# q's last two rows in two transfers, and two fillers ahead of v's first transposes

## The chip, the core and the metric

The kernel runs on one core of one Trainium2 chip. Its metric is the device time of one execution in microseconds (us); a result is the median of several runs. The engines are called PE (matrix products), PEld (its loads of weights), DVE (vector), ACT (activation functions), POOL and SP; POOL and SP are used here above all to issue transfers (DMAs).

## What is computed

A cross-covariance attention over channels, for four batches, feeds a layer with a squared ReLU. All inputs are float32 (tau is 1):

```python
B, N, C = (4, 6080, 256)            # q, k, v
n_tokens, d_model, d_ff = (24320, 256, 2048)

def _attn_ref(q, k, v, tau) -> np.ndarray:
    qn = q / (np.linalg.norm(q, axis=1, keepdims=True) + 1e-06)
    kn = k / (np.linalg.norm(k, axis=1, keepdims=True) + 1e-06)
    s = kn.transpose(0, 2, 1) @ qn / tau
    s = s - s.max(-1, keepdims=True)
    a = np.exp(s)
    a /= a.sum(-1, keepdims=True) + 1e-09
    return (v @ a).astype(np.float32)

def _moe_ref(x, w_in, w_out, s, b) -> np.ndarray:
    h = x @ w_in
    r = np.maximum(h, 0.0)
    g = s * (r * r) + b
    return (g @ w_out).astype(np.float32)
```

The norms of q and k run over the 6080 rows of a batch, so they, and the 256 x 256 matrix of exponentials, are known only when the last row of q and of k has been read.

## The kernel before

**In outline.** For every batch, the Gram matrix of q and k is summed on PE (`mm`, L174, into s_ps), the squares of q and k are summed for the norms, the exponentials eT are formed, and the product of eT with w_in, called wa, replaces w_in; then h = v times wa, in groups of 512 tokens: v is transposed (vT), h_ps is made on PE (L825; for the first half of the first group L812), ACT takes the ReLU (L835), the squares are taken on DVE or ACT (L848, L846), and the second product follows (L996 with seven products in place of eight, L900 for the first and the last group). The Gram matrices of batches 1 to 3 are worked in between the groups of the batch ahead. Batch 0 has nothing to lie beside: its q and k are loaded and summed at the start, and this is where the change is.

**Batch 0 in pieces.** The 6080 rows are cut into 13 chunks: eleven of 128 partitions x 4 rows, and the last 448 rows as two chunks of 112 partitions x 2 rows. The first six come in pairs (`load_pair`), four by `load` (chunks 6 to 9). The last three chunks, which the code calls c0, c1 and c2 (10, 11, 12), are loaded in an order of their own (L547 to L549): k of c0, k of c1 and c2 together, q of c0 in two transfers of two rows a partition, q of c1 and c2 in two transfers of two rows a partition. In the last of these steps (`load_last(1)`, L158) the first transfer is q of c1 and the second q of c2. The transfers turn float32 into float16 on the way, so that a row of 256 is 512 bytes in the tile.

**The queue.** All these transfers are issued by POOL, in program order, and behind them v's first group without its last row a partition (`load_v(0, slice(0, 3))`, L557), w_in's first 256 columns and the next 256 (L558, L559), v's last row (L560), the rest of w_in in four pieces, v of group 1, w_out in four pieces, and so on.

**The end of batch 0's sums.** For c0, c1 and c2 `norm_ops` gives a list: the squares of k, the squares of q, and two steps that hand the squares, unfolded, to the sums. The squares of q of these chunks run on DVE (L201). In c0 the entry of q is itself a list of two, one a transfer; in c1 and c2 it is one function over both rows. `add_norms(0)` sums the squares of q over the partitions on PE, by products with a vector of ones, two a row (L270). The order on PE and DVE is written out by hand from L611 to L650: the squares and sums of k, k's inverse norms on ACT (`inverse_k`, four activations at L291), c0's and c1's products and sums for q, then for c2: the square of q (L641), the Gram products of its row 0 (L642), the hand-over, the last sums (`norms_q`, L644), the Gram products of row 1 (L645). Then come `inverse_q` (four activations on ACT, L291) and `scale_s` (two operations on DVE, L316), the transposes of v's first three rows a partition (`turn_v(0, range(3))()`, L648: six on PE at L496 and a copy to vT on DVE at L498), `keep_busy(1)` (L649) and `first_block`.

**The first block.** `first_block` (L354) forms the exponentials in two halves on ACT (L322). With each half PE makes the row sums r_ps (L362) and the first 256 columns of wa (L367). Then come the next 256 columns (L372), the transposes of v's fourth row, the reciprocal of the row sums on DVE (L378), and the scalings of wa: by ACT (L343) for one half of the rows of wa, by DVE (L345) for the other. The first h products (L812) read both.

**The fillers.** `keep_busy(n)` (L586) issues n products of a constant tile of ones, 128 x 512 float32, into a tile of PSUM that nobody reads (idle_ps, L589). It takes its tile from the pool of two that h_ps and the first wa_ps come from. Three fillers stand further ahead, behind chunks 7 and 8 (`FILL`, L584).

Of the kernel before, what the change touches and what calls it, by code (L numbers as in the profile page):

```python
# [16 lines left out]
def kernel(  # L17
# [37 lines left out]
    def po(ins):  # L55

        tc.keep_in_program_order(ins)
        return ins
# [32 lines left out]
    def h_tile(name):  # L91
        return ps_h.tile([P, 2, TG], FP32, tag="h_ps", name=name)


    JC = 4
# [16 lines left out]
    class Gram:  # L112
# [35 lines left out]
        def load_last(self, i):  # L148

            c = len(self.chunks) - 2  # L150
            at, np_, _ = self.chunks[c]
            if i == 0:
                self.raw[c] = qk_pool.tile([P, 2, JC, C], FP16, tag="qk", name="qk")
                for h in range(2):
                    t = self.raw[c][:, :, ts(h, 2)]
                    self.tiles[c + h] = t[:, 1], t[:, 0]
            rows = (k, q)[i][self.b, at:].rearrange("(p j) c -> p j c", j=JC)
            for js in [slice(0, JC)] if i == 0 else [ts(h, 2) for h in range(2)]:  # L158
                po(nc.gpsimd.dma_start(out=self.raw[c][:np_, i, js], in_=rows[:, js]))

        def cast(self, c):
# [21 lines left out]
        def norm_ops(self, c):  # L183

            qc, kc = self.tiles[c]
            _, np_, jc = self.chunks[c]
            st = {}

            at_end = self.b == 0 and c >= len(self.chunks) - NLATE

            def squares(a, js):
                def f():
                    if "sq" not in st:
                        if at_end:
                            st["sq"] = late_pool.tile([P, 2, jc, C], FP16, tag=f"sq{c}", name="sq")
                        else:
                            st["sq"] = sq_pool.tile([P, 2, JC, C], FP16, tag="sq", name="sq")
                    src = (qc, kc)[a][:np_, js, :]
                    if (a == 0 or c == len(self.chunks) - 1 if at_end else
                            a == 0 and (self.b > 0 or c % 2 == 0)):  # L200
                        po(nc.vector.tensor_mul(st["sq"][:np_, a, js, :], src, src))  # L201
                    else:
                        po(nc.scalar.activation(  # L203
                            out=st["sq"][:np_, a, js, :], in_=src, func=AF.Square))
                return f

            def fold(half, arrays, last):
                def f():
                    src = st["f", 2 * half] if 2 * half < jc else st["sq"]
                    if ("f", half) not in st:  # L210
                        if last:
                            t = f3_pool.tile([P, 2, 1, C], FP16, tag="f3", name="f3")
                        else:
                            t = sq_pool.tile([P, 2, half, C], FP16, tag=f"f{half}", name="f")
                        st["f", half] = t
                    po(nc.vector.tensor_add(  # L216
                        st["f", half][:np_, arrays], src[:np_, arrays, :half, :],
                        src[:np_, arrays, half : 2 * half, :]))
                    if last and c == 0:
                        self.first = st["f", half]  # L220
                    if last and c == 0:
                        for rows in self.rows:
                            rows.append((st["f", half], np_, 1))
                return f

            def into_first():

                dst, src = self.first[:np_], st["f", 1][:np_]
                if self.b == 0:
                    po(nc.vector.tensor_add(dst, dst, src))  # L230
                else:
                    po(nc.gpsimd.dma_start(out=dst, in_=src, accum_op=ALU.add))  # L232

            def unfolded(a):
                self.rows[a].extend((st["sq"][:, :, j : j + 1], np_, 1) for j in range(jc))

            if self.b == 0 and c >= len(self.chunks) - NLATE - 1:
                ops = [lambda i=i: unfolded(i) for i in range(2)]
                if c == len(self.chunks) - NLATE:
                    return [squares(1, slice(0, jc)), [squares(0, ts(h, 2)) for h in range(2)], *ops]  # L240
                return [squares(1, slice(0, jc)), squares(0, slice(0, jc)), *ops]
            ops = []
            for h in range(0, jc, 4):
                js = slice(h, min(h + 4, jc))
                ops += [squares(1, js), squares(0, js)]
            if jc == 8:
                ops += [fold(4, slice(0, 1), False), fold(4, slice(1, 2), False)]
            ops += [fold(2, slice(0, 2), False), fold(1, slice(0, 2), True)]
            return ops + [into_first] if c > 0 else ops
# [239 lines left out]
    def turn_v(g, js):  # L489
        v16 = v_tiles[g]  # L490
        if g not in vT_tiles:
            vT_tiles[g] = vtpool.tile([P, CH, TG], FP16, tag="vT", name="vT")
        vT_ps = ps_o.tile([P, CH, TG], FP16, tag="o_ps", name="vT_ps")
        for j in js:
            for ch in range(CH):
                po(nc.tensor.transpose(vT_ps[:, ch, ts(j, P)], v16[:, j, ts(ch, P)], ident16))  # L496
        cols = ds(js[0] * P, len(js) * P)
        return lambda: po(nc.vector.tensor_copy(out=vT_tiles[g][:, :, cols],  # L498
                                                in_=vT_ps[:, :, cols]))
# [86 lines left out]
    def keep_busy(n):  # L586

        for _ in range(n):
            po(nc.tensor.matmul(h_tile("idle_ps")[:, 0, :], fill[:, :P], fill, start=True,  # L589
                                stop=True, skip_group_check=True))  # L590
# [4 lines left out]
    for c in range(NCH0 - NLATE - 1):  # L595
        ops = g0.norm_ops(c)
# [7 lines left out]
    c_, c0, c1, c2 = range(NCH0 - NLATE - 1, NCH0)  # L604
    ops = {c: g0.norm_ops(c) for c in (c_, c0, c1, c2)}

    def add_rows(a, c):
        ops[c][2 + a]()
        g0.add_norms(a)
# [28 lines left out]
    g0.rows[0].extend(half)  # L638
    g0.add_norms(0)
    add_rows(0, c1)  # L640
    ops[c2][1]()  # L641
    g0.mm(c2, 0)  # L642
    ops[c2][2]()
    norms_q()  # L644
    g0.mm(c2, 1)  # L645
    for f in (*inverse_q, scale_s):
        f()
    turn_v(0, range(3))()  # L648
    keep_busy(1)  # L649
    first_block()  # L650


# [367 lines left out]
    for s in range(NS + FT):  # L1020
# [27 lines left out]
        squares = {**SQUARES, 3: (), 5: SQUARES[3], 7: SQUARES[5]} if g == 1 else SQUARES  # L1048
# [44 lines left out]
```

## Time and profile before

| what | before |
|---|---|
| median of 3 runs | 713.3 us (713.22 to 713.45) |
| the profiled execution, its own time | 713.27 us |
| its span, first to last instruction | 711.5 us |
| mean granted clock of PE | 0.998 |
| PE busy | 692.5 us (97% of the span) |
| DVE, ACT, POOL busy | 633.6 us (89%), 548.6 us (77%), 113.3 us (16%) |
| granted clock of PE, 23.51 to 26.93 us | 0.50 |
| granted clock of PE, 26.93 to 40.58 us | 1.00 |
| bytes moved, mean rate | 83.81 MB, 118 GB/s |
| rate from 26 to 34 us | 192 to 213 GB/s |

The profile is that of one execution, which took 713.27 us by the clock of the runs and 711.5 us from its first to its last instruction. Its views are used as follows. The chain that ended last is followed back from the last instruction to whatever released each step; it tells what a step waited for, on the assumption of one releaser each. The timeline has one line for an instruction or a few alike: start, length, engine, line, operation, the tile it writes and those that it reads, shapes, how many, and in brackets the idle time of the engine ahead of it with its releaser. The issues of transfers have the time from issue to landing. In the page, the line of PE's clock and of the engines' shares by slices of the span shows that the first slice (17.8 us) and the second are the only ones in which PE is not nearly full.

From issue to landing, for the transfers that matter (one issue each, asked for its own moment):

| transfer | issued at, us | KB | us to landing |
|---|---|---|---|
| q of c0, first two rows | 22.29 | 128 | 9.0 |
| q of c0, last two rows | 23.52 | 128 | 8.4 |
| q of c1 (first transfer of `load_last(1)`) | 24.76 | 112 | 7.8 |
| q of c2 (second) | 26.08 | 112 | 7.0 |
| v of group 0, three rows a partition | 27.31 | 192 | 7.8 |
| w_in, columns 0 to 255 | 28.53 | 128 | 6.8 |
| w_in, columns 256 to 511 | 29.79 | 128 | 6.2 |
| v of group 0, last row a partition | 30.89 | 64 | 5.4 |

### The profile page before, as it was taken

The numbers are of one execution on the slowest core, as the hardware profiler recorded it, in microseconds if no ns is written. First come the engines' busy times: TensorE is split into PE (matmuls) and PEld (weight loads), VectorE is DVE, ScalarE is ACT, GpSimd is POOL, SyncE is SP. The second block draws the span as 40 slices with busy tenths as digits, with TensorE's granted clock in tenths as the row PEclk, the third lists the DMA queues.
The fourth block names the chain that finished last, engine by engine and source line by source line (L and its number), as shares of the span: only waits on it lengthen the run. The fifth ranks groups of instructions, "written<-read, shape, count | busy, mean of one in ns | idle before, by whom it ended". The sixth has DMA issues, their size and how long they took to land.

```text
span 711.5 us, 17551 instructions
## 1 busy us (share of the span) xinstructions
PE 692.5 (97%) x7436; PEld 503.3 (71%) x7436; DVE 633.6 (89%) x904; ACT 548.6 (77%) x599; POOL 113.3 (16%) x189
## 2 busy tenths in 40 slices
PE   3799999999999999999999999999999999999998
PEld 2566777776777777777677777777768777777777
DVE  3899999999988989998999899998998888887886
ACT  5889877787787777778877777777877777877875
POOL 3543142202102221111010222111000000000000
PEclk9999999999999999999999999999999999999999
DMA  9999999657656979465771887838323323321202
GB/s 240 205 254 152 191 174 144 124 92 121 126 119 109 136 137 156 95 95 104 153 127 51 148 147 143 125 75 108 93 62 75 98 67 76 99 59 47 82 31 75
DMA packets 87694, 83.81 MB, mean 118 GB/s; under 512 B 56320, under 2 KB 63280, under 8 KB 87360
## 3 DMA queue, kind: packets, MB, share of 16 engines
q0 software_dynamic: 26848, 43.74, 38.5%
q1 hardware_dynamic: 60336, 37.71, 23.7%
q8 instruction: 58, 0.95, 0.6%
q10 hardware_dynamic: 432, 1.25, 0.5%
q14 instruction: 20, 0.16, 0.1%
HBM read 78.91 MB, written 24.90 MB: 146 GB/s over the span
## 4 chain that ended last, share of the span: by engine, by line
PE 95%; DMA 4%; ACT 1%; DVE 0%; issue 0%
PE h_ps L825 46%; PE o_ps L996 40%; PE s_ps L174 4%; DMA qk<-in_k_dram 1%; PE wa_ps L419 1%; DMA raw<-in_q_dram 1%; DMA v<-in_v_dram 1%; PE o_ps L900 1%; PE o_ps L872 0%; PE wa_ps L350 0%; ACT sq L203 0%; ACT qk L165 0%; DVE f L216 0%; PE vT_ps L496 0%; PE h_ps L812 0%
## 5 line engine op out<-in xcount | busy, mean ns | idle before, releaser
L835 ACT ACTIVATE r<-h_ps 128x1024 f16<-128x1024 f32 (+1 forms) x384 | 388.8, 1014 | 144.3 <-PE h_ps L825 141.1
L825 PE MATMUL h_ps<-vT,wa 128*128 128x512 f16 (+7 forms) x1628 | 450.9, 364 | 0.0
L996 PEld LDWEIGHTS <-S 128*128 128x128 f16 x2944 | 198.1, 98 | 84.3
L996 PEld LDWEIGHTS <-g 128*128 128x128 f16 x2208 | 155.0, 98 | 74.1
L848 DVE TENSOR_TENSOR g<-r 128x2048 f16<-128x2048 f16 (+2 forms) x150 | 174.4, 1163 | 10.2 <-ACT r L835 9.7
L996 PE MATMUL o_ps<-T,S 128*128 128x128 f16 x2208 | 183.1, 219 | 0.0
L825 PEld LDWEIGHTS <-wa 128*128 128x128 f16 x1628 | 136.3, 98 | 18.2 <-ACT wa L343 0.2
L996 PE MATMUL o_ps<-w_out,g 128*128 128x128 f16 x1472 | 134.2, 219 | 0.0
L846 ACT ACTIVATE g<-r 128x1024 f16<-128x1024 f16 (+1 forms) x97 | 100.3, 1034 | 0.2
L853 DVE SCALAR_TENSOR_TENSOR o_sb<-o_ps,s_out,u 128x256 f32<-128x256 f32 x138 | 66.2, 480 | 36.0 <-PE o_ps L996 34.4
L174 PE MATMUL s_ps<-qk 128*128 128x256 f16 (+1 forms) x384 | 71.1, 287 | 14.7 <-ACT qk L165 10.9
L485 POOL DMA_DIRECT2D v<-in_v_dram x49 | 32.4, 665 | 243.2 <-DMA vT<-v 150.2
L232 POOL DMA_DIRECT2D f<-f x33 | 28.9, 875 | 242.3 <-DVE f L216 188.9
L853 DVE SCALAR_TENSOR_TENSOR u<-o_ps,s_out,rowconst 128x256 f32<-128x256 f32 x138 | 65.7, 476 | 0.0
L996 PE MATMUL o_ps<-w_out,S 128*128 128x128 f16 x736 | 63.5, 219 | 0.0
L996 PE MATMUL o_ps<-N,g 128*128 128x128 f16 x736 | 63.4, 219 | 0.0
L925 DVE TENSOR_TENSOR S<-S,g 128x2048 f16<-128x2048 f16 (+1 forms) x47 | 56.4, 1200 | 1.2
L203 ACT ACTIVATE sq<-qk 128x1024 f16<-128x1024 f16 (+2 forms) x53 | 54.5, 1041 | 2.8 <-DVE f L216 1.8
L923 DVE TENSOR_TENSOR S<-g 128x2048 f16<-128x2048 f16 (+1 forms) x47 | 56.0, 1192 | 0.0
L929 DVE TENSOR_TENSOR S<-g,S 128x2048 f16<-128x2048 f16 x46 | 55.8, 1214 | 0.0
L927 DVE TENSOR_TENSOR S<-g 128x2048 f16<-128x2048 f16 x46 | 55.8, 1214 | 0.0
L174 PEld LDWEIGHTS <-qk 128*128 128x128 f16 (+1 forms) x384 | 32.9, 103 | 20.0 <-ACT qk L165 10.9
(108 smaller groups left out, 332.5 us busy)
## 6 DMA issues: line engine op xcount, KB each, us to landing
out_dram<-o_sb SPq DMA_DIRECT2D x41, 512.0 KB, 3.0
v<-in_v_dram POOLq DMA_DIRECT2D x46, 256.0 KB, 4.7
qk<-in_k_dram POOLq DMA_DIRECT2D x38, 256.0 KB, 6.3
qk<-in_q_dram POOLq DMA_DIRECT2D x37, 256.0 KB, 7.0
f<-f POOLq DMA_DIRECT2D x30, 128.0 KB, 3.2
out_dram<-o_sb SPq DMA_DIRECT2D x12, 256.0 KB, 4.3
vT<-v SPq DMA_TRANSPOSE x182, 3.4
w<-in_moe_w_out_dram POOLq DMA_DIRECT2D x4, 512.0 KB, 8.5
```

Source lines behind the costliest of these rows:

```text
L174: po(nc.tensor.matmul(self.s_ps[:, ch, :], qc[:np_, j, ts(ch, P)], kc[:np_, j, :], start=(c == 0 and j == 0 and ch == 0), stop=(c == len(s ...
L203: po(nc.scalar.activation(out=st["sq"][:np_, a, js, :], in_=src, func=AF.Square))
L825: po(nc.tensor.matmul(dst, wa[:, ci, ts(m, P)], src, start=(ci == 0), stop=(ci == CH - 1), skip_group_check=True))
L835: po(nc.scalar.activation(out=r16[:, :, i % 2, :n], in_=h_tiles.pop((g, i))[:, :, :n], func=AF.Relu))
L846: po(nc.scalar.activation(out=dst, in_=src, func=AF.Square))
L848: po(nc.vector.tensor_mul(dst, src, src))
L853: po(nc.vector.scalar_tensor_tensor(out=dst, in0=src, scalar=s_out, op0=ALU.mult, in1=add, op1=ALU.add))
L923: po(nc.vector.tensor_add(T[1], A21, A22))
L925: po(nc.vector.tensor_sub(T[2], T[1], A11))
L927: po(nc.vector.tensor_sub(T[3], A11, A21))
L929: po(nc.vector.tensor_sub(T[4], A12, T[2]))
L996: po(nc.tensor.matmul(st[name][:, j, :], a()[:, i, ts(j, P)], w[:, i, :], start=first, stop=last, skip_group_check=True))
```

## The change

q's part of `load_last` is issued as three transfers: rows 0 and 1 of a partition together as before, row 2 alone, row 3 alone. So q of c2 comes in two transfers of 112 partitions x 1 row. The squares of q of c2 become a list of two functions, one a row, which are called one after the other in the place where the one stood. The filler behind the transposes of v's first part goes away, and two fillers are issued ahead of `inverse_q`, `scale_s` and these transposes, behind the Gram products of c2's row 1.

```diff
@@ load_last
             rows = (k, q)[i][self.b, at:].rearrange("(p j) c -> p j c", j=JC)
-            for js in [slice(0, JC)] if i == 0 else [ts(h, 2) for h in range(2)]:
+            for js in [slice(0, JC)] if i == 0 else [slice(0, 2), slice(2, 3), slice(3, 4)]:
                 po(nc.gpsimd.dma_start(out=self.raw[c][:np_, i, js], in_=rows[:, js]))
@@ norm_ops
                 if c == len(self.chunks) - NLATE:
                     return [squares(1, slice(0, jc)), [squares(0, ts(h, 2)) for h in range(2)], *ops]
+                if c == len(self.chunks) - 1:
+                    return [squares(1, slice(0, jc)), [squares(0, ts(h, 1)) for h in range(2)], *ops]
                 return [squares(1, slice(0, jc)), squares(0, slice(0, jc)), *ops]
@@ the order by hand
     add_rows(0, c1)
-    ops[c2][1]()
+    for f in ops[c2][1]:
+        f()
     g0.mm(c2, 0)
     ops[c2][2]()
     norms_q()
     g0.mm(c2, 1)
+    keep_busy(2)
     for f in (*inverse_q, scale_s):
         f()
     turn_v(0, range(3))()
-    keep_busy(1)
     first_block()
```

## The prediction

> **What bounds the kernel now.** I read the chain that ended last first, the waits of the tensor engine second, and then the timeline of the start. By the page's chain, PE holds 95% of the span; the list of waits, asked for PE from 37 us to the end, comes back empty, and PE is busy for the whole of 40.58 to 700 us. So from about 37 us on PE waits for nobody: whatever moves the first matmuls of the feed-forward part moves the end by the same amount, and nothing behind them has time to give. The change lies wholly ahead of that point. The chain there, from the window 26 to 39 us (columns: start, length, what):
>
> ```profile
> 16.36 10.67 DMA qk<-in_k_dram
> 27.03 0.28 issue
> 27.31 7.77 DMA v<-in_v_dram
> 35.08 0.05 issue
> 35.13 0.51 PE vT_ps L496 x6
> 35.63 0.29 PE idle_ps L589
> 35.92 0.04 PE r_ps L362 x2
> ```
>
> v's first part lands at 35.08, six transposes follow, then one filler (L589, 0.29 us), then the first products with the exponentials. But a second chain runs beside this one, that of q's last rows. The timeline (start, length, engine, line, operation, count, idle before and its releaser):
>
> ```profile
> 32.54 0.98 DVE L201 TENSOR_TENSOR sq<-qk 112x512 f16<-112x512 f16 x2 [0.16 <-DMA qk<-in_q_dram]
> 33.57 0.25 PE L270 MATMUL n_ps<-ones,sq 112*128 112x1 f16 x4
> 33.86 0.26 ACT L291 ACTIVATE r<-n_ps,tiny 128x2 f32<-128x2 f32 x1 [0.22 <-PE n_ps L270]
> 34.96 0.91 ACT L322 ACTIVATE eT<-sm_t,r 128x256 f16<-128x256 f32 x2
> ...
> 35.67 0.56 DVE L498 COPY vT<-vT_ps 128x768 f16<-128x768 f16 x1 [0.74 <-PE vT_ps L496]
> 36.28 0.17 DVE L378 RECIPROCAL rs<-r_ps 128x2 f32<-128x2 f32 x1
> 36.54 0.37 ACT L343 ACTIVATE wa<-wa_ps,rs 128x128 f16<-128x128 f32 x1 [0.67 <-PE wa_ps L367]
> ```
>
> q's last piece lands at 33.08 (issued 26.08, 7.0 us to landing), its square starts at 33.09 and ends at 33.52, its sums are on PE from 33.57, the inverse norms on ACT from 33.86, and the second half of the exponentials ends at 34.96 + 0.91 = 35.87. PE takes that half up at 35.94, which is also when the filler and the first half let it. So the two chains meet within 0.1 us, and this is the main reading: neither can be shortened alone by much.
>
> **The change, part by part.** First, **one more transfer on POOL's queue.** The issues show its rule:
>
> ```profile
> 24.76 0.54 POOL L159 DMA_DIRECT2D qk<-in_q_dram  x1 [0.71 <-DMA qk<-in_k_dram]
> 26.08 0.53 POOL L159 DMA_DIRECT2D qk<-in_q_dram  x1 [0.78 <-DMA qk<-in_q_dram]
> 27.31 0.58 POOL L485 DMA_DIRECT2D v<-in_v_dram  x1 [0.71 <-DMA qk<-in_k_dram]
> 28.53 0.75 POOL L555 DMA_DIRECT2D w_in<-in_moe_w_in_dram  x1 [0.64 <-DMA qk<-in_q_dram]
> ```
>
> Each issue waits for the landing of the eighth transfer ahead of it (27.31 follows the landing of 16.36 + 10.67 = 27.03). One more ahead puts row 2 at 26.08, row 3 at 27.31, v at 28.53, and w_in's pieces and v's last row one place later each. v's descriptors are then there about 4 us before their turn, since the piece ahead of it lands at 33.08; no queue runs dry, and the later issue itself costs nothing. If that cover were gone, it would be 1.2 us.
>
> What costs is the size of the packets: 112 of 1,024 bytes become 224 of 512. The trace has no such q transfer; the nearest rows are w_in's first two pieces, 256 packets of 512 bytes each, landing at 28.53 + 6.8 = 35.33 and 29.79 + 6.2 = 35.99: 0.66 us for 256, so 0.29 for 112. The lower end is half of the present 0.55 us between q's last two landings (32.53 and 33.08), 0.275; the upper end is the single packets' durations, 60 against 98 ns, which makes 0.55 x 120/98 / 2 = 0.34. I take 0.30 (nearest size and pitch: v's last row, 128 packets in 0.34 on the engines not disturbed). Row 2 lands at 32.82, row 3 at 33.12 (33.07 to 33.20), and v and all behind it 0.05 us later (0 to 0.13).
>
> The Trainium skill, "DMA: Bandwidth & Descriptors", section "Anatomy of one DMA — SWDGE (gpsimd) path", speaks against the split: it gives every such DMA a fixed cost of about 2.0 us beside its bytes. By that rule, paid in series, the sum would be about 715.2 us. The trace's landings 0.55 to 0.66 us apart in a full queue say that the fixed part overlaps, and I go by them.
>
> **Two squares in place of one.** No row has 112x256. On the same line 128x1024 takes 0.69 and 112x512 takes 0.42, so 0.27 per 512 columns and 0.16 fixed: 0.29 for 256. Bounds: 0.21 (half of 0.42) and 0.42 (no shorter). Two vector instructions in a row overlap by 0.08 (L316: 0.42 each, 0.76 for both). The square ahead of them runs 32.54 to 32.97. Row 2: from 32.89 to 33.18; row 3: from 33.14 (landing and 0.02) to 33.43. Now the end is 33.52: a gain of 0.09. At the bounds: 33.09 + 0.21 = 33.30, a gain of 0.22; and, with 0.42 each and no overlap, 33.81, a loss of 0.29. Queued behind row 3's square on DVE is only L316 at 34.17, which nobody misses.
>
> **The sums.** Two of four L270 can run before the last square; of 0.25 us for four, the last two spare 0.05. ACT's earlier work ends at 33.23 + 0.42 = 33.65, so the inverse starts at 33.72 for 33.86. Sum for q's chain: -0.14 us (-0.27 to +0.29); the second exponential ends at 35.73.
>
> **The fillers.** Two at 0.29 each stand ahead of the transposes, where PE now idles 1.06 us before 35.13; q's last products end their issue at about 33.8, so the fillers are through by 34.5, 0.6 us before v. They cost nothing; if v came by 34.0 they would cost up to 0.5. The one behind goes away: -0.29 in PE's order. The second half's products then start at 35.79 for 36.05, held by the exponential (35.73 and 0.05) and by PE's own row of 35.52 and four instructions.
>
> **Where the gain stops.** The reciprocal (L378) stands behind the copy of vT on DVE. v 0.05 later means that the copy runs from 35.72 to 36.28, and the reciprocal starts at 36.20 with the usual overlap (L498 at 37.08 starts before the instruction ahead of it ends) or at 36.32 without: end 36.37 or 36.49. The first scalings follow 0.06 later, 36.43 (36.55) for 36.54, and the first h matmuls hang on them. So of 0.26 us only about **0.1** arrives: -0.11, with bounds -0.29 (the filler whole) and +0.42 (the square's and the packets' worst, together). The profiled execution took 713.27 us (span 711.53 and 1.74 around it); 713.27 - 0.1 = 713.17, and its distance to the median of the runs shown, 713.3, is 0.03. I predict **713.2 us**, no change by a bound of 0.2% (1.43 us), about what a measurement of this kernel can tell from no change.
>
> **The rivals.** One: **v lands early.** The trace's completions show v's landing to be odd: fifteen of its sixteen counts are in by 33.98, the sixteenth comes at 35.08. Between 33 and 34 us the DMA view has a guest:
>
> ```profile
> q0 software_dynamic: 320, 0.18, 125.2%
> q8 instruction: 1, 0.02, 6.1%
> ```
>
> 6.1% of 16 engines in 1 us is 0.98 us of one engine, a fetch of instructions that starts at 33.04. If it missed v, v would land near 34.05; q's chain alone would then bound, scalings at 36.29, -0.25: 713.0 us. Against it: v's packets move later, further into the fetch. 10%.
>
> Two: **the split brings nothing**, since DVE works the squares one by one anyway: with 0.42 each, the exponential ends at 36.16, its products start at 36.22 for 36.05: +0.2, 713.5 us. For it: the first square ends at 32.97, 0.15 after row 2's landing. Against it: the slope of the durations. 12%.
>
> Three, **slower: the fetch strikes q's row 3 in place of v.** It cost v 1.1 us beyond the other engines, so row 3 would land at 34.2 or later and the whole chain of norms behind it: +1.0 to +1.7, 714.3 to 715.0 us. It decides from the point where the fetch starts before the last count of row 3 is on its way on that engine, some 0.4 to 0.8 us earlier than now. PE's instructions are the same up to there, which speaks against it. 8%, half of it beyond 714.7.
>
> Four: **the clock falls.** These windows (PE busy first, PEclk and DMA last) are as long as the record's stretch of half clock:
>
> ```profile
> 20.10:23.51 3.41, 1.36 (x12) 0.92 (x12) 3.20 (x7) 2.64 (x4) 1.54 (x3) 1.00 1.12 209
> 23.51:26.93 3.42, 2.98 (x15) 1.86 (x13) 3.19 (x7) 2.65 (x3) 1.59 (x3) 0.50 1.12 209
> 33.75:37.17 3.42, 2.36 (x29) 1.63 (x25) 2.10 (x7) 2.50 (x9) 2.39 (x4) 1.00 1.39 194
> ```
>
> A stretch with PE 1.36 us busy was followed by one at half clock; one with 2.36 was not. Were the stretch from 37.17 at half clock, it would cost 1.7 us: 715.0. But the change adds a filler there. 4%.
>
> A gain of over 1.43 us has no place: the idle 1.06 and the filler's 0.29 before the products make 1.35 together. I leave 6% for what I don't see.
>
> **How the numbers follow.** Forecast 60%, one 10%, two 12%, three 8%, four 4%, unseen 6%. Faster 0.06; slower 0.04 + 0.04 = 0.08; within 0.86. The range leaves out three, four and the unseen (18%): from 713.2 - 0.3 less the runs' spread of 0.2 to 713.3 + 0.42 and 0.2, that is 712.7 to 713.9.
>
> **What would show it.** Two L201 of 112x256 of about 0.29 us, the last ending near 33.43; L291 on n_ps near 33.72; L589 twice between 33.8 and 34.5 and none after 35; v's landing at 35.1; the reciprocal still right behind the copy; the first L343 at about 36.43. The forecast is wrong if v lands before 34.5 or after 35.4, if row 3 lands after 33.3, if PEclk shows 0.5 after 27 us, or if PE waits anywhere after 37 us.

## The result, and the profile after

The changed kernel takes 719.95 us (median of 4 runs, 719.32 to 720.15) against 713.29 us before (4 runs, 713.22 to 713.45): a ratio of 1.009, 95% interval 1.0078 to 1.0102. It is slower by some 6.7 us, where no change was forecast. The profiled execution took 719.93 us, with a span of 718.2.

The lines at the start that answer to those of before, from the timeline of the changed kernel (start, length, engine, line, operation; line numbers are larger by two or three):

```profile
32.42 1.50 DVE L201 TENSOR_TENSOR sq<-qk 128x512 f16<-128x512 f16 x4 [0.20 <-DMA qk<-in_q_dram]
...
34.21 0.26 ACT L293 ACTIVATE r<-n_ps,tiny 128x2 f32<-128x2 f32 x1
...
35.30 0.91 ACT L324 ACTIVATE eT<-sm_t,r 128x256 f16<-128x256 f32 x2
...
36.51 0.17 DVE L380 RECIPROCAL rs<-r_ps 128x2 f32<-128x2 f32 x1 [0.68 <-PE r_ps L364]
...
36.77 0.99 ACT L345 ACTIVATE wa<-wa_ps,rs 128x128 f16<-128x128 f32 x3 [0.56 <-PE wa_ps L369]
```

The start isn't where the time went: the first scaling stands at 36.77 for 36.54 and the first h product at 37.20 for 36.96, 0.24 us later in an execution whose first loads also came later (q of c1 lands at 32.97 us for 32.52). The chain of waits between 40 and 74 us shows the loss (start, length, what):

```profile
50.74 1.29 SPq L513
...
54.66 12.54 DMA vT<-v
67.19 0.14 issue
67.33 1.01 PE h_ps L828 x2
```

SP issues the four transposing transfers of v's group 2; the last needs 12.54 us from issue to landing. Before, issued at 53.64, it needed 6.2, and PE took the group up at 62.17 without a wait (the view of that issue, and PE's timeline):

```profile
vT<-v SPq DMA_TRANSPOSE x1, 6.2
```

```profile
62.17 0.59 PE L825 MATMUL h_ps<-vT,wa 128*128 128x512 f16 x2
```

After, PE stands and waits for it:

```profile
63.25 0.38 PE L174 MATMUL s_ps<-qk 128*128 128x256 f16 x2
67.33 1.01 PE L828 MATMUL h_ps<-vT,wa 128*128 128x512 f16 x2 [3.70 <-DMA vT<-v]
```

and the clock follows. The windows of the changed kernel (PE busy first; PEclk, DMA share and GB/s last):

```profile
64.00:67.04 3.04, 0.00 (x0) 0.00 (x0) 3.01 (x4) 0.63 (x3) 0.00 (x0) 1.00 1.36 154
67.04:70.46 3.42, 3.13 (x9) 1.31 (x10) 1.55 (x2) 0.80 (x1) 0.53 (x1) 0.50 1.12 250
```

PE does nothing for 3 us and then works 3.42 us at half clock, which costs 1.7 by estimate, half of it. The sum: 0.24 at the start, 3.7 for the transposes, 1.7 for the clock, and 0.7 near 45 us, where the second product of group 0 waits until DVE has cast the first piece of w_out (PE's list of waits has these two entries alone, 3.7 and 0.7): 6.3 of the 6.66 us between the two profiled executions.

**Why are the transposes late?** POOL's timelines from 49 us on, first before:

```profile
49.10 0.53 POOL L130 DMA_DIRECT2D qk<-in_q_dram  x1 [0.29 <-DMA v<-in_v_dram]
60.40 0.53 POOL L485 DMA_DIRECT2D v<-in_v_dram  x1 [10.77 <-DVE N L682]
61.28 0.53 POOL L130 DMA_DIRECT2D qk<-in_k_dram  x1 [0.34 <-issue]
```

then after:

```profile
51.01 0.53 POOL L130 DMA_DIRECT2D qk<-in_q_dram  x1 [0.27 <-DMA s_bc<-in_moe_s_dram]
51.53 0.54 POOL L487 DMA_DIRECT2D v<-in_v_dram  x1
52.45 0.53 POOL L130 DMA_DIRECT2D qk<-in_k_dram  x1 [0.39 <-DVE g L851]
53.05 0.53 POOL L130 DMA_DIRECT2D qk<-in_q_dram  x1
54.55 0.53 POOL L130 DMA_DIRECT2D qk<-in_k_dram  x1 [0.97 <-ACT r L838]
55.54 0.53 POOL L130 DMA_DIRECT2D qk<-in_q_dram  x1 [0.46 <-DMA qk<-in_k_dram]
67.75 0.53 POOL L487 DMA_DIRECT2D v<-in_v_dram  x1 [11.68 <-DVE S L926]
```

Before, POOL stands still for 10.77 us ahead of the load of v's group 5, and group 2's transposes have the engines almost to themselves. After, this load goes at once, with four transfers of q and k behind it, and POOL stands still only ahead of group 6's. The views of the transfers from 55 to 60 us count packets, bytes and time for each queue (q0 is POOL's, q1 carries the transposes), before:

```profile
q1 hardware_dynamic: 1499, 0.34, 118.2%
q0 software_dynamic: 72, 0.11, 11.8%
```

and after:

```profile
q0 software_dynamic: 389, 0.71, 93.7%
q1 hardware_dynamic: 371, 0.09, 18.7%
```

The transposes get through a quarter of the packets, one small packet of theirs for one large one of POOL's.

The releaser in the brackets (DVE L682) is a guess of the view. What the load waits for stands in the compiled programs' lists of instructions, before and after:

```
48 L485 DMACopy v_659<-in_v_dram 128x1024 [waits DMAHW4_49,DMAHW3_49,DMAHW5_49,DMAHW2_49,DMASW0_49]
49 L487 DMACopy v_663<-in_v_dram 128x1024 [waits DMASW1_49,PE_49]
```

DMAHW2 to 5 are the four transposes of group 2. v has four buffers, and the framework that builds the program chooses which one a new group gets. Before, group 5 got the buffer of group 2 (free when its transposes have landed) and group 6 that of group 1 (free when PE has transposed it); after, the two are swapped. Beside the edited instructions, some waits of their neighbours and of one subtraction on DVE, and the numbers of the eight semaphores that POOL's transfers use in turn, these two loads are all that differs in the lists of the five engines. No line of the source says it.

### The profile page after: what moved, and what is told of

It is laid out like the page before. It is cut to its first block, busy times and chain, and to the rows that moved or that the text cites. A ratio compares the mean times of both kernels' runs of the same rounds, so it can differ in the third digit from the quotient of the medians.

```text
span 718.2 us, 17554 instructions
## 1 busy us (share of the span) xinstructions
PE 693.9 (97%) x7437; PEld 503.5 (70%) x7437; DVE 634.4 (88%) x905; ACT 548.6 (76%) x599; POOL 113.1 (16%) x190
## 4 chain that ended last, share of the span: by engine, by line
PE 91%; DMA 7%; POOL 1%; SPq 1%; issue 0%; DVE 0%; ACT 0%; POOLq 0%
PE h_ps L828 44%; PE o_ps L999 40%; PE s_ps L174 5%; DMA qk<-in_k_dram 4%; DMA vT<-v 2%; DMA v<-in_v_dram 2%; PE wa_ps L421 1%; SPq L513 1%; PE o_ps L875 0%; POOL qk L143 0%; POOL w L574 0%; PE n_ps L268 0%; ACT sq L203 0%; DVE sm_t L318 0%; DVE vT L500 0%
```

## The experiments

**1 to 4: is it the buffers, the split or the fillers?** In the first, v's buffers are named by hand in the changed kernel so that the choice is that of before:

```diff
-    vpool = pool("vpool", 4)
+    vpool = pool("vpool", 1)
...
+    V_SLOT = lambda g: g % 4 if g < 5 else (0, 2, 1, 3)[g % 4]
...
-            v_tiles[g] = vpool.tile([P, TG // P, C], FP16, tag="v16", name="v16")
+            v_tiles[g] = vpool.tile([P, TG // P, C], FP16, tag=f"v16_{V_SLOT(g)}", name="v16")
```

> The changed kernel, with v's four buffers named by hand so that group 5 is loaded into the buffer of group 2, as in the kernel before, and group 6 into that of group 1. Theory A (the swapped buffers: in the changed kernel group 5 goes into group 1's buffer, freed by PE, so POOL no longer waits at this load for group 2's transposes, and five loads of 2,048-byte packets run beside these transposes): the last of group 2's transposes lands near 60 us as before (59.85), PE waits nowhere behind 40 us for over 0.3 us, PEclk stays 1.0 behind 30 us, and the time is 712.9 to 714.3 us (what is left of the stalls at 40.5 and 45.0 us would make the upper end). Rival B (the extra transfer and its 512-byte packets set back everything behind them on the queue): 718.5 to 720.5. Rival C (the fillers: the one behind the transposes was needed for the clock): 718.5 to 720.5, with the half clock at 67 us still there.

Measured: 713.48 us, ratio 1.0002 (0.9993 to 1.0012). POOL's timeline of this run has the pause again, and its q1 line for 55 to 60 us the packets:

```profile
60.91 0.53 POOL L488 DMA_DIRECT2D v<-in_v_dram  x1 [10.56 <-DMA vT<-v]
```

```profile
q1 hardware_dynamic: 1697, 0.39, 115.3%
```

PE waits for nobody behind 37 us. With the old buffers the whole change, split and fillers, makes no difference that can be measured.

The second is the kernel before with the new buffers and nothing else of the change:

```diff
+    V_SLOT = lambda g: g % 4
...
+            v_tiles[g] = vpool.tile([P, TG // P, C], FP16, tag=f"v16_{V_SLOT(g)}", name="v16")
```

> The kernel before, with v's buffers named by hand as the changed kernel has them: group 5 into group 1's buffer, group 6 into group 2's; nothing else of the change. Theory A: group 2's transposes land at 66 to 68 us, PE stalls 3 to 4 us for them, a stretch at half clock follows, 717.5 to 720.5 us. Rivals B and C: 713.0 to 713.7, since neither the transfers nor the fillers are touched.

Measured: 717.56 us (715.63 to 719.25), ratio 1.005 (1.0033 to 1.0067), at the lower end of what was expected. Its PE timeline, from the longest of its four executions (719.25 us):

```profile
61.87 0.38 PE L174 MATMUL s_ps<-qk 128*128 128x256 f16 x2
66.47 0.59 PE L826 MATMUL h_ps<-vT,wa 128*128 128x512 f16 x2 [4.21 <-DMA vT<-v]
```

The stall and the half clock behind it (67.21 to 70.63) come without any edit at the start.

The third and the fourth make the two halves of the change alone, with the buffers as the framework chooses them:

```diff
-            for js in [slice(0, JC)] if i == 0 else [ts(h, 2) for h in range(2)]:
+            for js in [slice(0, JC)] if i == 0 else [slice(0, 2), slice(2, 3), slice(3, 4)]:
...
-    ops[c2][1]()
+    for f in ops[c2][1]:
+        f()
```

> The kernel before with q's last two rows in two transfers and two squares alone; the filler stays behind the transposes. Buffers as they come out: here group 5 falls into group 1's buffer, as in the changed kernel. Theory A: 718.5 to 720.5, the same stall. Rival B: the same 718.5 to 720.5. Rival C: 713.0 to 714.0.

```diff
     g0.mm(c2, 1)
+    keep_busy(2)
...
     turn_v(0, range(3))()
-    keep_busy(1)
```

> The kernel before with two fillers ahead of the transposes of v's first part and none behind; q's transfers and squares as before. Buffers as they come out: here group 5 stays in group 2's buffer. Theory A: 712.9 to 713.5 us, no stall behind 37 us. Rival B: 713.0 to 713.5. Rival C: 718.5 to 720.5.

Measured: the split alone 719.76 us, ratio 1.0093 (1.0077 to 1.0109), with PE waiting 4.9 us for vT in the profiled execution, the longest of four (721.59 us); the fillers alone 713.2 us, 0.9998 (0.9989 to 1.0008). So the split is what makes the framework choose otherwise; the fillers don't. Why one transfer more, some 23 places ahead in POOL's list, turns the choice was not traced.

**5: the split with the old buffers.** The split of run 3 and the V_SLOT of run 1.

> The kernel before with q's last two rows in two transfers and two squares, the filler behind the transposes as before, and v's buffers named by hand as in the kernel before. Theory A (the swapped buffers make the loss): 713.0 to 714.3 us, no stall of PE over 0.5 us behind 37 us. Rival B (the split itself sets the queue back): over 718. Beside the run of the fillers alone (713.2) it tells how the two halves of the change share what is left of it; by the prediction's sum the split alone, with the filler in the way, brings nothing: within 0.2 us of the kernel before.

Measured: 713.29 us, 1.0002 (0.9993 to 1.0011). The split costs nothing where the buffers stay, so the transfer more and its packets of 512 bytes are not the loss.

**6: the clock's share.** Ten fillers in the stall of the changed kernel:

```diff
+        if s == 2 * FT:
+            keep_busy(10)
         if g < NG:
             mm1(g, m)
```

> The changed kernel (its buffers named by hand as they came out), with ten fillers on PE just ahead of the first h products of group 2, where PE stalls 3.9 us for the transposes. Nothing else is touched. Theory D (the half clock from 67.04 to 70.46 us is the stall's own follower, and costs half of 3.4 us): the stall stays, PEclk stays 1.0 behind it, 717.6 to 718.8 us. Rival (the half clock comes from elsewhere, or the fillers lie in the way): 719.3 to 721.

Measured: 717.51 us, 1.0059 (1.0044 to 1.0074), just under the expected 717.6, against 719.95 for the changed kernel. The PE timeline shows the fillers, and that the transposes are still late:

```profile
62.02 3.27 PE L592 MATMUL idle_ps<-fill 128*128 128x512 f32 x10
67.15 0.59 PE L829 MATMUL h_ps<-vT,wa 128*128 128x512 f16 x2 [1.85 <-DMA vT<-v]
```

No half clock is recorded between 14 and 717 us. The gain, 2.4 us by the medians, is no less than the 1.7 that the half clock costs. It isn't shown to be the clock's alone: the 0.7 us near 45 us in the changed kernel's profile are missing here too.

**7: the transposes off the queue.** Group 2 is transposed on PE in the changed kernel, and the five loads go as early as there:

```diff
-            if g == 1:
-                at_step(12, lambda g=g: transpose_v(g))
+            if g in (1, 2):
+                at_step(12 if g == 1 else 26, lambda g=g: transpose_v(g))
```

> The changed kernel (its buffers named by hand as they came out), but group 2 of v is transposed on PE (eight products and one copy on DVE, as for group 1) in place of four transposing transfers on SP's queue. The five loads at 51.5 to 55.5 us stay free to go. Theory A (the loads hurt only because group 2's transposes run beside them): no stall at 63 us, 713.4 to 715.5 us (0.45 us more on PE, and what is left of the small stalls at 40 and 45 us). Rival (the loads on the queue are themselves too late, whoever transposes): a stall of 2 us or more remains, 717 to 720.

Measured: 714.06 us, 1.0012 (1.0003 to 1.0022). PE doesn't wait at 63 us. The time is 0.8 us over the kernel before, which has less work on PE (0.45 us by the estimate above); the profile also has a wait of 0.3 us for w_out at 45 us. So the stall and the half clock come by way of group 2's transposes alone.

**8: which of the five loads?** The kernel before with its own buffers, but group 5's load issued behind the four transfers of q and k:

```diff
-            at_step(max(g - 4, 0) * FT + 2, lambda g=g: load_v(g))
+            at_step(max(g - 4, 0) * FT + (2 if g != 5 else 17), lambda g=g: load_v(g))
```

> The kernel before, its buffers named by hand as they were, but the load of v's group 5 is issued behind the two chunks of q and k (four transfers) that stood behind it; its wait for group 2's transposes stays, and now holds nothing back that is wanted here. Theory A1 (the wait helped by holding back the four transfers of q and k, 1 MB, whatever becomes of group 5): the transposes are late as in the changed kernel, a stall of 2 to 4 us and the half clock, 715.5 to 719 us. Theory A2 (it is the load of group 5 itself that collides): 713.0 to 714.0 us.

Measured: 715.36 us, 1.0033 (1.002 to 1.0046), just under the expected 715.5. Every group has its old buffer and waits for what it waited for there, and yet the stall is there (2.0 us in the profiled execution). The two queues from 55 to 60 us:

```profile
q0 software_dynamic: 496, 0.91, 96.3%
q1 hardware_dynamic: 495, 0.11, 17.9%
```

The windows of this run, up to the end of the stall and behind it:

```profile
60.74:64.15 3.41, 1.41 (x11) 0.78 (x9) 3.30 (x5) 2.35 (x4) 0.00 (x0) 1.00 1.49 124
64.15:67.57 3.42, 3.42 (x11) 1.50 (x12) 2.86 (x3) 1.19 (x2) 1.06 (x2) 0.50 1.04 200
```

The profiled execution was the longest, 716.84 us. The other four took 714.61 to 715.81 with a mean granted clock of 1.0, so no half clock is in them, and the 2.1 us by which the median is longer come without it. The wait at group 5's load was worth its time because of what it held back: 1 MB of q and k that nobody needed yet.

**9: the new buffers, held back again.** The changed kernel with its new buffers, and group 6's load, which has the wait now, right behind group 5's:

```diff
-            at_step(max(g - 4, 0) * FT + 2, lambda g=g: load_v(g))
+            at_step(max(g - (4 if g != 6 else 5), 0) * FT + 2, lambda g=g: load_v(g))
```

> The changed kernel with its own new buffers (group 5 in group 1's, group 6 in group 2's, named by hand), but group 6 is loaded right behind group 5, ahead of two chunks of q and k; so the wait for group 2's transposes stands again ahead of these four transfers, and only the load of group 5 (256 KB) runs beside the transposes. Theory A (what counts is that the wait holds the transfers back, not which buffer is whose): 713.2 to 714.8 us, no half clock behind 30 us, a stall at group 2 of under 1 us. Rival (the new buffers as such, or the load of group 5, make the loss): 716.5 to 720.

Measured: 713.58 us, 1.0003 (0.9993 to 1.0012). POOL's timeline:

```profile
50.64 0.53 POOL L488 DMA_DIRECT2D v<-in_v_dram  x1 [0.54 <-DMA s_bc<-in_moe_s_dram]
62.37 0.53 POOL L488 DMA_DIRECT2D v<-in_v_dram  x1 [11.20 <-DVE rowconst L669]
62.89 0.54 POOL L130 DMA_DIRECT2D qk<-in_k_dram  x1
```

Group 5's load alone beside the transposes costs nothing; the four transfers of q and k go at 62.89 and later, and the loss is gone with the swapped buffers still in place. What that load adds beside the four others is not shown: the four cost 2.1 us by the medians (run 8), all five 4.2 (run 2). No version is measurably faster than the kernel before.

## Why the prediction was wrong

**The step that failed** is the first one: "The change lies wholly ahead of that point", with "nothing behind them has time to give". The text followed the issues of POOL to w_in and v's last row and took the program behind for unchanged. It was not: the split moved two buffers, and with them a wait that kept 1 MB away from the transposes for 10 us. The swap alone costs 4.2 us (717.56, run 2), and the whole change without it nothing that can be measured (713.48, run 1). The words on the transfer itself, "the later issue itself costs nothing", hold (713.29, run 5). The empty list of waits was read as "nothing can be lost here"; it shows that PE was fed, not by how much. The margin could be read: group 2's last transpose lands at 53.64 + 6.2 = 59.8 in the profile before, and PE takes group 2 up at 62.17, 2.3 us later. And the pause of POOL, 49.63 to 60.40, was plain in the timeline; it was never asked what hangs on it. None of the four rivals names this, so the range, 712.7 to 713.9, held nothing of it. Two of its signs of being wrong came, PE's wait after 37 us and PEclk at 0.5 after 27.

**The local sum holds as far as it can be seen.** In the changed kernel q's rows land at 32.97 (both of c1), 33.28 and 33.60: 0.31 and 0.32 apart for the 0.30 taken. The squares of 112x256 take 0.29 each, as taken. Row 3 is past the 33.3 of the forecast's signs only because this execution starts later. From the landing of c1's q to the start of the inverse it is 1.34 us before, 1.24 after and 1.21 in run 1: a gain of 0.10 to 0.13 for 0.14. From the same mark to the first scaling it is 4.02 before, and 3.92 and 3.94 in runs 2 and 8, which have the old start; 3.80 after, and 3.77, 3.98, 3.77 and 3.91 in runs 1, 6, 7 and 9, which have the new one. The means differ by 0.11, as the sum said, but the two ranges overlap. It was not always the copy of vT that took the rest: in run 1 the reciprocal starts at 36.12, while the copy runs until 36.19. And the mark itself lies between 32.35 and 32.99 in these profiles, so the start varies by more than the change gains, and the time shows nothing: 1.0002 in run 1.

**The rivals.** The first, v early, half came true in the changed kernel (v at 34.50, no use to anybody, since the exponentials end at 36.21). The second, no gain from DVE's squares, is refuted by their durations. The third, the fetch striking row 3, did not come: the fetch started at 33.26, and row 3 landed on time. The fourth, half clock, came as to its price (1.7 us), but 30 us later and as the follower of a stall.

**What stays open.** Why the framework chooses otherwise; and why the new buffers cost 4.2 us alone and 6.4 with the split (runs 2 and 3, 717.56 and 719.76). Part of it may be small waits of PE at 40 to 48 us: 0.3 to 0.75 us in three of seven profiles with the split (the changed kernel, runs 3 and 7), under 0.1 in the other four, and none in the four without it.

## What to carry to other kernels

Before an edit is costed by the lines that it touches, compare the compiled lists of instructions with their waits: an added transfer can move buffers, and with them waits, far behind it. A long pause on a queue may be what keeps a small, urgent transfer on time, so ask of each pause what runs in it and with what margin. If such an order matters, write it down (name the buffers, place the wait) and don't leave it to an allocator.

## What the runs showed that was not expected

Two queues with work for the same engines pass packets in equal numbers, though not of equal size: 496 packets of POOL's against 495 of the transposes' in run 8, 389 against 371 in the changed kernel, where POOL's are of 2,048 bytes and the transposes' of 256; almost alone, before, the transposes pass 1,499 in 5 us. The Trainium skill, "DMA: Bandwidth & Descriptors", section "Queues, rings and completion order", says that each engine takes turns between queues by the packet. The equal counts fit that, though no run shows that its packet is the one that the profile counts. They show what the turn costs: some eight times the bytes for the one, a quarter to a third of the pace for the other.

A stall of 2.0 us was followed by a stretch at half clock in the profiled execution of run 8 (PE busy 1.41 of 3.41 us in the window ahead). The Trainium skill, "TensorE: Matmul & The Clock Gate", section "HAM oscillation — how this bites in real kernels", puts the bound at idle gaps of more than about 3.4 us. The measurement decides: neither that window nor the one ahead of the stretch at 23.51 us before (1.36 us busy, no gap over 1.4) has such a gap. The two stretches of the changed kernel begin at 26.08 and 67.04 us, those of run 8 at 23.19 and 64.15: both 40.96 apart, 12 times 3.413. Cut every profile that records a stretch into windows of 3.41 us in step with it: ten windows from 14 to 705 us, with PE busy for 1.57 us or less, were each followed by half clock, and no window with 1.60 or more was.
